# Batch 0 of a linear-attention and gated-FFN kernel worked in pairs of heads in place of halves, with a third of one weight loaded earlier

## The chip, the cores and the metric

The kernel runs on one core of a Trainium2 chip. The metric is the device time of one launch in microseconds (us), so lower is better. Five engines work side by side, each through its own list of instructions in a fixed order: TensorE (PE in the profile) multiplies matrices and transposes; VectorE (DVE) and ScalarE (ACT) work element by element; GpSimd (POOL) casts and issues the transfers of weights and of batches 1 to 7; SyncE (SP) issues the loads of batch 0 and the stores. Data moves between HBM and the on-chip SBUF by DMA; matmul results land in PSUM.

## The reference

Linear attention without softmax over 8 batches of 8 heads, 576 tokens and 64 channels, then a normalisation, then a gated feed-forward layer on the 4608 tokens of 512 channels. Inputs and output are 32-bit floats.

```python
# _attn_ref: q, k, v are (8, 8, 576, 64)
kv = np.einsum('bhsd,bhse->bhde', k, v)
out = np.einsum('bhsd,bhde->bhse', q, kv)
rms = np.sqrt(np.mean(out * out, axis=-1, keepdims=True) + 1e-06)
x = out / rms * g_norm                       # then heads side by side: (4608, 512)

# _moe_ref: w_gate, w_val (512, 1536); w_out (1536, 512); w_res (512, 512)
g = x @ w_gate
gelu = 0.5 * g * (1.0 + erf(g * inv_sqrt2))
val = x @ w_val
ffn_out = gelu * val @ w_out
res_gate = 1.0 / (1.0 + np.exp(-(x @ w_res)))
return x + res_gate * ffn_out
```

## The kernel before

Each batch gives a block of 512 tokens (4 tiles of 128, index j); its last 64 tokens ("rem", "last") are gathered, two batches to a tile, in a ninth block. A block's feed-forward part, which the slots below number, is twelve column blocks f of gate and value (`m_gval`), four residual tiles (`m_res`), and the product with w_out; in block 0 that product runs by twelve steps f over all four tiles (`out_by_f`). The attention of batch b + 1 is put amid the slots of block b. Batch 0 has nothing to hide behind: its q, k and v are loaded in two halves of four heads as 32-bit floats, cast on the engines, and worked through (k'v, q times it, norm, transposes) half after half, with the first two column blocks taken up as parts of x get ready (`first_gval`). Short matmuls on zeros (`keep_warm`) fill TensorE's waits. All other loads are cast in the transfer, issued by GpSimd in one row: weights of gate and value in four chunks of 256, 256, 512 and 512 columns, then w_res, batch 1, and w_out in thirds.

```python
    def load_batch(b):
        tiles_16(b)
        raw[b, "q"] = stage.tile([P, H, NJ * D], FP16, tag="qraw", name="qraw")
        raw[b, "k"] = stage.tile([P, H, NJ * D], FP16, tag="kraw", name="kraw")
        nc.gpsimd.dma_start(out=raw[b, "q"], in_=rows4(q, b, 0, H))
        nc.gpsimd.dma_start(out=raw[b, "k"], in_=rows4(k, b, 0, H))
        nc.gpsimd.dma_start(out=b16_t[b, "v"], in_=rows4(v, b, 0, H))
        load_last_kv(b)
        load_qr(b)
# ... (cut)
    def by_token(b, which):
        nc.vector.tensor_copy(
            out=b16_t[b, which].rearrange("p j h d -> p h j d"),
            in_=raw[b, which].rearrange("p h (j d) -> p h j d", j=NJ),
        )
# ... (cut)
    def load_wo(f0, f1):
        nc.gpsimd.dma_start(
            out=wo16[:, f0:f1, :], in_=moe_w_out[f0 * P : f1 * P, :].rearrange("(ff p) c -> p ff c", p=P)
        )
# ... (cut)
    def a_kv(b, lo, hi):
        if lo == 0:
            st[b]["kvp"] = pattn.tile([P, NP, P], FP32, tag="at", name="kvp")
        ps = st[b]["kvp"]
        for pr in range(lo, hi):
            kv_steps(b, ps[:, pr, :], pr)
        if hi == NP:
            nc.vector.tensor_tensor(
                out=st[b]["kv2"], in0=ps, in1=mask[:, None, :].to_broadcast([P, NP, P]), op=ALU.mult
            )

    def a_ss(b, j, ps):
        sq = attnp.tile([P, H, D], FP32, tag="sq", name="sq")
        nc.scalar.activation(out=sq, in_=ps, func=AF.Square)
        nc.vector.tensor_reduce(out=st[b]["ss"][:, j, :], in_=sq, op=ALU.add, axis=mybir.AxisListType.X)
# ... (cut)
    def a_o(b, j):
        s = st[b]
        ps = pattn.tile([P, C], FP32, tag="at", name="op")
        for pr in range(NP):
            nc.tensor.matmul(
                ps[:, pr * P : (pr + 1) * P], lhsT=s["qT"][:, j, pr, :], rhs=s["kv2"][:, pr, :], start=True, stop=True
            )
        a_ss(b, j, ps)
        s["o"][j] = ps
# ... (cut)
        nc.scalar.copy(out=qtr[0][:, :, 0:R], in_=ps[:, :, 0:R])
        nc.scalar.copy(out=qtr[1][:, :, R : 2 * R], in_=ps[:, :, R : 2 * R])

    def a_rem_o(b):
        # ... (cut: matmuls with both batches' kv2, copy, a_ss)
# ... (cut)
    def m_gval(blk, f):
        if f == 0:
            hids[blk] = hidp.tile([P, NF, NJ * P], FP16, tag="hid", name="hid")
        gps = pmoe.tile([P, NJ * P], FP32, tag="mm", name="gps")
        m_mm(gps, wg_c, f, blk, 0, NJ)
        vps = pmoe.tile([P, NJ * P], FP32, tag="mm", name="vps")
        m_mm(vps, wv_c, f, blk, 0, NJ)
        m_act(blk, f, gps, vps)
# ... (cut)
    def out_by_f(blk):

        ths, fpss, pfs = [], [], []
        slots = [lambda j=j: ths.append(m_res(blk, j)) for j in range(NJ)]

        def step(f):
            if f == 0:
                fpss.extend(pmoe.tile([P, C], FP32, tag="mm", name="fps") for _ in range(NJ))
            for j in range(NJ):
                m_ffn(blk, j, f, fpss[j])
            if f == NF - 1:
                pfs.extend(m_gate(ths[j], fpss[j]) for j in range(NJ))

        slots += [lambda f=f: step(f) for f in range(NF)]
        return slots, [lambda j=j: m_store(blk, j, pfs[j]) for j in range(NJ)]
# ... (cut)
    def load_first(which, t, half):
        hs = slice(half * HH, (half + 1) * HH)
        nc.sync.dma_start(out=raw[0, which][:, hs, :], in_=rows4(t, 0, hs.start, hs.stop))
# ... (cut)
    for half in range(2):
        load_first("q", q, half)
        load_first("k", k, half)
        load_first_last(0, half)
        load_first_last(1, half)
        load_first("v", v, half)
# ... (cut)
    def f_cast_last(half):
        hs = slice(half * HH, (half + 1) * HH)
        for i in range(2):
            nc.gpsimd.tensor_copy(out=last_kv[0][i][0:R, hs, :], in_=last_raw[i][:, hs, :])
# ... (cut)
    f_cast("q", 0, HH, nc.scalar.copy)
    f_qT(0)
    f_cast("k", 0, HH, nc.vector.tensor_copy)
    f_qT_out(0, nc.scalar.copy)
    f_qT_out(1, nc.scalar.copy)
    nc.vector.tensor_copy(out=g16, in_=gps)
    f_cast_last(0)
    f_cast("v", 0, HH, nc.vector.tensor_copy)
    keep_warm(7)
    f_kv(0)
    f_kv_out(0)
    f_cast("q", HH, H, nc.scalar.copy)
    keep_warm(2)
    f_o(0, 0, 2, pmoe, "mm")
    f_o(0, 2, 2, pmoe, "mm")

    hold = consts.tile([1, 1], FP16, name="hold")
    nc.gpsimd.tensor_copy(out=hold, in_=s0["kv2"][0:1, 0, 0:1])
    load_wg(0)
    load_wv(0)
    f_cast("k", HH, H, nc.gpsimd.tensor_copy)
    f_cast_last(1)
    for i in range(1, len(WCS)):
        load_wg(i)
        load_wv(i)
    f_sq(0, 0, 2)
    f_sq(0, 2, 2)
    f_red(0, 0, 2)
    # ... (cut: squares, sums, norm, transposes of the first half amid k'v of the second)
# ... (cut)

        hids[0] = hidp.tile([P, NF, NJ * P], FP16, tag="hid", name="hid")
        tiles = [pmoe.tile([P, NJ * P], FP32, tag="mm", name=n) for n in ("gps", "vps", "gps", "vps")]

        def part(j0, j1, c0, c1):
            for f in range(2):
                m_mm(tiles[2 * f], wg_c, f, 0, j0, j1, c0, c1)
                m_mm(tiles[2 * f + 1], wv_c, f, 0, j0, j1, c0, c1)

        part(0, 2, 0, 2)
        f_xT_pe(0, 2, 2)
        # ... (cut: the second half tile by tile, then the rest of the four products)
        for f in range(2):
            m_act(0, f, tiles[2 * f], tiles[2 * f + 1])
        load_qr(0)
# ... (cut)
        plan = {
            NF - 1: [lambda: by_token(b, "q")],
            NF: [lambda: by_token(b, "k")],
            NF + 3: [
                lambda: attn_begin(b),
                lambda: a_qT(b, 0),
                lambda: a_qT(b, 1),
                lambda: load_batch(b + 1),
                lambda: a_kv(b, 0, NP),
                lambda: a_rem_qT(b),
            ],
            NF + 4: [lambda: a_rem_o(b), o[0]],
            NF + 5: [o[1]],
            NF + 6: [o[2]],
            NF + 7: [o[3]],
            NF + 8: [lambda: a_norm(b), t[0], t[1], t[2], t[3], t[4]],
            2 * NF + 1: [x[0], x[1]],
            2 * NF + 2: [x[2], x[3]],
            2 * NF + 3: [x[4]],
        }
# ... (cut)
            if blk == 0 and s == 2:
                nc.gpsimd.dma_start(out=wr16, in_=moe_w_res.rearrange("(cc p) c -> p cc c", p=P))
                load_batch(1)
                for f in range(0, NF, 4):
                    load_wo(f, f + 4)
```

Of the kernel before, what the change touches and what calls it, by code (L numbers as in the profile page):

```python
# [18 lines left out]
def kernel(  # L19
# [15 lines left out]
    nc = tc.nc  # L35
# [391 lines left out]
    def load_first(which, t, half):  # L427
        hs = slice(half * HH, (half + 1) * HH)
        nc.sync.dma_start(out=raw[0, which][:, hs, :], in_=rows4(t, 0, hs.start, hs.stop))
# [11 lines left out]
    for half in range(2):  # L441
        load_first("q", q, half)
        load_first("k", k, half)
        load_first_last(0, half)
        load_first_last(1, half)
        load_first("v", v, half)
# [44 lines left out]
    def f_cast(which, lo, hi, copy):  # L491
        hs = slice(lo, hi)
# [9 lines left out]
    def f_cast_last(half):  # L502
        hs = slice(half * HH, (half + 1) * HH)
        for i in range(2):
            nc.gpsimd.tensor_copy(out=last_kv[0][i][0:R, hs, :], in_=last_raw[i][:, hs, :])

    def f_qT(half):
        q16 = b16_t[0, "q"].rearrange("p j h d -> p j (h d)")
        for e2 in range(2):
            pr = 2 * half + e2  # L510
            first["qT", pr] = ps = pattn.tile([P, NJ, P], FP16, tag="at", name="qtp")
            for j in range(NJ):
                nc.tensor.transpose(ps[:, j, :], q16[:, j, pr * P : (pr + 1) * P], ident)
# [4 lines left out]
    def f_kv(half):  # L518
        first["kv", half] = ps = pattn.tile([P, 2, P], FP32, tag="at", name="kvp")
        for e2 in range(2):  # L520
            kv_steps(0, ps[:, e2, :], 2 * half + e2)

    def f_kv_out(half):
        nc.vector.tensor_tensor(
            out=s0["kv2"][:, 2 * half : 2 * half + 2, :],
            in0=first["kv", half],
            in1=mask[:, None, :].to_broadcast([P, 2, P]),
# [3 lines left out]
    def f_o(half, j0, n, pool, tag):  # L531

        first["o", half, j0] = ps = pool.tile([P, n, HH * D], FP32, tag=tag, name="op")
        for j in range(n):
            for e2 in range(2):
                pr = 2 * half + e2
                nc.tensor.matmul(
                    ps[:, j, e2 * P : (e2 + 1) * P],
                    lhsT=s0["qT"][:, j0 + j, pr, :],
                    rhs=s0["kv2"][:, pr, :],  # L540
                    start=True,
                    stop=True,
                )

    def f_sq(half, j0, n):
# [295 lines left out]
```

## Time and profile before

The median of three runs is 356.24 us (356.02 to 356.77); the profiled execution spans 354.6 us.

| engine | busy us | share of the span | instructions |
|---|---|---|---|
| TensorE matmul | 343.0 | 97% | 1905 |
| TensorE weight load | 168.9 | 48% | 1905 |
| VectorE | 214.1 | 60% | 428 |
| ScalarE | 125.7 | 35% | 215 |
| GpSimd | 47.7 | 13% | 74 |

The page's lines name engine, source line and tiles as "out<-in". Busy time of TensorE's matmuls is modelled at its ends and overlaps from one to the next, so 97% is the share in which some matmul was under way, not a share of the peak. A table by stage gives for each stretch its length, then for PE, PE's weight loads, DVE, ACT and POOL the busy time and the instructions, then TensorE's granted clock (1.00 is full speed), the share of DMA engines busy (over 1 where two transfers overlap on an engine) and GB/s moved; bytes of a casting transfer are counted as written, at 16 bits. In the chain of waits each line has the start, the length and the instruction or transfer that held the end back.

### The profile page before, as it was taken

Reading aid. Unit: us, or ns where it says so; the run is one execution under the profiler, and the core shown is the slowest. Engines: PE = TensorE matmul, PEld = TensorE weight load, DVE = VectorE, ACT = ScalarE, POOL = GpSimd, SP = SyncE. Lnnn points to the kernel's source line nnn. Section 1 sums busy time; section 2 is a strip of 40 time slices with the busy share of each in tenths; the row PEclk is TensorE's granted clock in tenths of the full one; section 3 lists DMA queues with packets and bytes.
Section 4 is the critical chain, followed back from the end, with each engine's and each line's share of the span. In section 5 each row is a group of like instructions: output and inputs, shape, how many; then the busy total and the mean of one; then the engine's idle time right before and its main releaser. Section 6 shows DMA issues by size and latency. Waiting matters only on the chain.

```text
span 354.6 us, 5021 instructions
## 1 busy us (share of the span) xinstructions
PE 343.0 (97%) x1905; PEld 168.9 (48%) x1905; DVE 214.1 (60%) x428; ACT 125.7 (35%) x215; POOL 47.7 (13%) x74
## 2 busy tenths in 40 slices
PE   6879999999999999999999999999999999999995
PEld 2554465454454445544554445444544444444443
DVE  5655448868757774676569656865587543343433
ACT  3653474253146222531363125422542233223320
POOL 1853330050050005000130023000000000000000
PEclk9999999999999999999999999999999999999999
DMA  8999999489699058904594369327000500020013
GB/s 250 221 180 201 193 203 142 137 137 106 160 164 131 2 133 167 153 0 118 136 166 36 86 169 175 24 61 194 0 2 30 133 31 0 30 87 5 1 31 89
DMA packets 77707, 37.95 MB, mean 107 GB/s; under 512 B 42226, under 2 KB 73202, under 8 KB 77682
## 3 DMA queue, kind: packets, MB, share of 16 engines
q0 software_dynamic: 39792, 17.70, 39.7%
q1 hardware_dynamic: 37728, 19.80, 20.6%
q8 instruction: 15, 0.25, 0.3%
q10 hardware_dynamic: 162, 0.13, 0.1%
q14 instruction: 10, 0.08, 0.1%
HBM read 38.80 MB, written 9.44 MB: 136 GB/s over the span
## 4 chain that ended last, share of the span: by engine, by line
PE 84%; DMA 9%; POOL 2%; DVE 1%; SPq 1%; ACT 0%; issue 0%; DVEq 0%
PE fps L348 25%; PE gps L315 23%; PE vps L315 23%; PE rps L335 8%; DMA wv<-in_moe_w_val_dram 4%; DMA wo<-in_moe_w_out_dram 4%; PE op L194 2%; PE kvp L165 2%; DMA vf<-in_v_dram 1%; POOL wg L120 1%; PE fps L377 1%; POOL wv L120 1%; PE orp L212 1%; PE kvp L172 0%; SPq L435 0%; DVE hid L304 0%
## 5 line engine op out<-in xcount | busy, mean ns | idle before, releaser
L315 PE MATMUL gps<-xT,wg 128*128 128x512 f16 (+2 forms) x448 | 112.3, 371 | 2.3 <-ACT xT L597 1.2
L304 DVE TENSOR_TENSOR hid<-ge,vps 128x512 f16<-128x512 f16 x108 | 73.5, 685 | 65.8 <-PE vps L315 59.3
L315 PE MATMUL vps<-xT,wv 128*128 128x512 f16 (+2 forms) x448 | 112.3, 371 | 0.0
L303 ACT ACTIVATE ge<-gps 128x512 f16<-128x512 f32 x108 | 64.4, 598 | 114.3 <-PE gps L315 105.2
L348 PE MATMUL fps<-wo,hid 128*128 128x512 f16 x420 | 96.9, 379 | 0.6 <-DMA wo<-in_moe_w_out_dram 0.6
L315 PEld LDWEIGHTS <-wv 128*128 128x128 f16 x448 | 43.4, 98 | 50.4 <-DMA wv<-in_moe_w_val_dram 0.3
L348 PEld LDWEIGHTS <-hid 128*128 128x128 f16 x420 | 40.8, 98 | 48.7 <-DMA wo<-in_moe_w_out_dram 0.8
L315 PEld LDWEIGHTS <-wg 128*128 128x128 f16 x448 | 42.0, 98 | 44.0 <-issue 2.7
L354 DVE SCALAR_TENSOR_TENSOR pf<-th,fps 128x512 f32<-128x512 f32 x35 | 23.8, 686 | 47.6 <-PE fps L348 47.6
L344 ACT ACTIVATE th<-rps 128x512 f32<-128x512 f32 x36 | 21.5, 598 | 79.5 <-PE rps L335 79.5
L335 PE MATMUL rps<-wr,xT 128*128 128x512 f16 x144 | 36.5, 379 | 0.0
L188 DVE TENSOR_REDUCE ss<-sq 128x8 f32<-128x512 f32 x32 | 21.5, 683 | 7.3 <-ACT sq L187 5.5
L359 DVE SCALAR_TENSOR_TENSOR osb<-pf,t 128x512 f32<-128x512 f32 x35 | 24.2, 691 | 1.1
L335 PEld LDWEIGHTS <-xT 128*128 128x128 f16 x144 | 14.1, 98 | 17.0
L187 ACT ACTIVATE sq<-op 128x512 f32<-128x512 f32 x28 | 16.7, 598 | 9.9 <-PE op L194 9.2
L727 POOL COPY hold<-qT 1x1 f16<-1x1 f16 x5 | 0.9, 177 | 138.2 <-DMA qT<-q 138.2
L252 DVE TENSOR_TENSOR t<-op,ny 128x512 f16<-128x512 f32 x28 | 17.8, 680 | 0.1
L271 DVE TENSOR_TENSOR t<-t,g 128x512 f16<-128x512 f16 x36 | 13.3, 417 | 0.0
L165 PE MATMUL kvp<-v,k 128*128 128x128 f16 x128 | 10.6, 219 | 2.4 <-DVE v L495 2.2
L165 PEld LDWEIGHTS <-k 128*128 128x128 f16 x128 | 8.9, 98 | 6.3 <-DVE v L495 1.9
L194 PEld LDWEIGHTS <-qT 128*128 128x128 f16 x112 | 8.4, 98 | 5.7
L194 PE MATMUL op<-kv,qT 128*128 128x128 f16 x112 | 10.8, 219 | 0.0
(96 smaller groups left out, 168.0 us busy)
## 6 DMA issues: line engine op xcount, KB each, us to landing
out_dram<-osb SPq DMA_DIRECT2D x32, 256.0 KB, 2.4
qraw<-in_q_dram POOLq DMA_DIRECT2D x7, 512.0 KB, 6.1
kraw<-in_k_dram POOLq DMA_DIRECT2D x7, 512.0 KB, 8.3
v<-in_v_dram POOLq DMA_DIRECT2D x7, 512.0 KB, 10.1
wo<-in_moe_w_out_dram POOLq DMA_DIRECT2D x3, 512.0 KB, 14.0
qf<-in_q_dram SPq DMA_DIRECT2D x2, 512.0 KB, 4.7
kf<-in_k_dram SPq DMA_DIRECT2D x2, 512.0 KB, 5.8
vf<-in_v_dram SPq DMA_DIRECT2D x2, 512.0 KB, 6.0
```

Of the source, the lines that this page charges most:

```text
L165: nc.tensor.matmul(ps, lhsT=k16[:, j, cs], rhs=v16[:, 2 * pr : 2 * pr + 2, j * D : (j + 1) * D], start=(j == 0), stop=False,)
L188: nc.vector.tensor_reduce(out=st[b]["ss"][:, j, :], in_=sq, op=ALU.add, axis=mybir.AxisListType.X)
L194: nc.tensor.matmul(ps[:, pr * P : (pr + 1) * P], lhsT=s["qT"][:, j, pr, :], rhs=s["kv2"][:, pr, :], start=True, stop=True)
L252: nc.vector.tensor_tensor(out=t_t[blk][:, jj, :].rearrange("p (h d) -> p h d", h=H), in0=s["o"][j].rearrange("p (h d) -> p h d", h=H), in1 ...
L303: nc.scalar.activation(out=ge, in_=gps, func=AF.Gelu)
L304: nc.vector.tensor_tensor(out=hids[blk][:, f, :], in0=ge, in1=vps, op=ALU.mult)
L315: nc.tensor.matmul(ps[:, j0 * P : j1 * P], lhsT=w[:, cc, :], rhs=xT_t[blk][:, j0:j1, cc, :], start=(cc == 0 and j0 == 0), stop=(cc == NP - ...
L335: nc.tensor.matmul(rps, lhsT=xT_t[blk][:, j, cc, :], rhs=wr16[:, cc, :], start=(cc == 0), stop=(cc == NP - 1),)
L344: nc.scalar.activation(out=th, in_=rps, func=AF.Tanh, scale=0.5)
L348: nc.tensor.matmul(fps, lhsT=hids[blk][:, f, j * P : (j + 1) * P], rhs=wo16[:, f, :], start=(f == 0), stop=(f == NF - 1))
L354: nc.vector.scalar_tensor_tensor(out=pf, in0=th, scalar=1.0, in1=fps, op0=ALU.add, op1=ALU.mult)
L359: nc.vector.scalar_tensor_tensor(out=osb, in0=pf, scalar=0.5, in1=t_t[blk][:, j, :], op0=ALU.mult, op1=ALU.add)
```

## The change

Batch 0's q, k and v are loaded by pairs of heads (four pairs), and each step of its attention is done by pair, in an order written out as a row of words; a word names the step, the pair, for some the half of the token tiles (a or b), and the engine: qc, kc, vc and lc cast q, k, v and the last rows; qT and qo transpose q and copy it out; kv and kvo are k'v and its mask; o is q times it; sq, rd, rt, ri, t are square, sum, root, reciprocal and normalised x; xT and xo transpose x and copy it out; g and v are a pair's share of the first two gate and value column blocks; w issues a weight chunk, gelu loads ScalarE's table. So the norm of one pair runs beside the loads and casts of the next, and the first column blocks take up x pair by pair. The aim is that less work is left when the last of v has landed. GpSimd no longer waits for the first k'v before it issues weights, and casts parts of pair 2 itself. The first third of w_out is moved ahead of batch 1's loads, and the attention of batch 1 is put some slots later.

```diff
-    def load_first(which, t, half):
-        hs = slice(half * HH, (half + 1) * HH)
+    def load_first(which, t, pr):
+        hs = slice(2 * pr, 2 * pr + 2)
         nc.sync.dma_start(out=raw[0, which][:, hs, :], in_=rows4(t, 0, hs.start, hs.stop))
# ... (cut)
-    for half in range(2):
-        load_first("q", q, half)
-        load_first("k", k, half)
-        load_first_last(0, half)
-        load_first_last(1, half)
-        load_first("v", v, half)
+    for pr in range(NP):
+        load_first("q", q, pr)
+        load_first("k", k, pr)
+        if pr % 2 == 0:
+            load_first_last(0, pr // 2)
+            load_first_last(1, pr // 2)
+        load_first("v", v, pr)
# ... (cut)
+    tiles = {}
+    engines = {"A": nc.scalar.copy, "D": nc.vector.tensor_copy, "P": nc.gpsimd.tensor_copy}
+
+    def of_pair(pr):
+        return slice(2 * pr, 2 * pr + 2), slice(pr * P, (pr + 1) * P)
+
+    def f_cast(which, pr, copy):
# ... (cut)
+    def f_cast_last(half, copy):
         hs = slice(half * HH, (half + 1) * HH)
         for i in range(2):
-            nc.gpsimd.tensor_copy(out=last_kv[0][i][0:R, hs, :], in_=last_raw[i][:, hs, :])
-
-    def f_qT(half):
+            copy(out=last_kv[0][i][0:R, hs, :], in_=last_raw[i][:, hs, :])
# ... (cut)
+    def f_qT(pr):
         q16 = b16_t[0, "q"].rearrange("p j h d -> p j (h d)")
-        for e2 in range(2):
-            pr = 2 * half + e2
-            first["qT", pr] = ps = pattn.tile([P, NJ, P], FP16, tag="at", name="qtp")
-            for j in range(NJ):
-                nc.tensor.transpose(ps[:, j, :], q16[:, j, pr * P : (pr + 1) * P], ident)
+        first["qT", pr] = ps = pattn.tile([P, NJ, P], FP16, tag="at", name="qtp")
+        for j in range(NJ):
+            nc.tensor.transpose(ps[:, j, :], q16[:, j, of_pair(pr)[1]], ident)
# ... (cut)
+    def f_kv(pr):
+        first["kv", pr] = ps = pattn.tile([P, P], FP32, tag="at", name="kvp")
+        kv_steps(0, ps, pr)
+
+    def f_kv_out(pr):
+        nc.vector.tensor_tensor(out=s0["kv2"][:, pr, :], in0=first["kv", pr], in1=mask, op=ALU.mult)
# ... (cut)
+    def f_o(pr):
+        pool, tag = (pmoe, "mm") if pr < 2 else (pattn, "at")
+        first["o", pr] = ps = pool.tile([P, NJ, P], FP32, tag=tag, name="op")
+        for j in range(NJ):
+            nc.tensor.matmul(
+                ps[:, j, :], lhsT=s0["qT"][:, j, pr, :], rhs=s0["kv2"][:, pr, :], start=True, stop=True
+            )
+
+
+    def f_sq(pr, j0, j1):
+        first["sq", pr, j0] = sq = attnp.tile([P, j1 - j0, 2, D], FP32, tag=f"sq{j1 - j0}", name="sq")
+        ps = first["o", pr].rearrange("p j (h d) -> p j h d", h=2)
+        nc.scalar.activation(out=sq, in_=ps[:, j0:j1], func=AF.Square)
# ... (cut)
+    def f_mm(ws, i, pr, j0, j1):
+
+        for f in range(2):
+            if (f, i) not in tiles:
+                tiles[f, i] = [pmoe.tile([P, NJ * P], FP32, tag="mm", name="gv"[i] + "ps"), 0]
+            ps, done = tiles[f, i]
+            tiles[f, i][1] = done = done + j1 - j0
+            nc.tensor.matmul(
+                ps[:, j0 * P : j1 * P],
+                lhsT=w_of(ws, f)[:, pr, :],
+                rhs=xT0[:, j0:j1, pr, :],
+                start=(done == j1 - j0),
+                stop=(done == NP * NJ),
# ... (cut)
+    def f_piece(word):
+
+        name = word.rstrip("0123abADP")
+        rest = word[len(name) :]
+        # ... (cut: each word runs one step; "qc0A" casts q of pair 0 on ScalarE, D is VectorE, P is GpSimd)
# ... (cut)
+    opening = """
+    qc0A qT0 kc0D qo0A lc0P warm2 vc0D kv0 qc1A kvo0 kc1D o0 qT1 warm2 vc1D sq0 qc2P kv1 rd0 qo1A warm1 kvo1
+    kc2P rt0 qT2 o1 ri0 qo2D lc1P sq1 warm3 w0 t0 vc2A rd1 xT0 kv2 warm1 qc3A kvo2 qT3 rt1 o2 kc3D xo0A ri1 warm2
+    vc3D sq2 t1 w1 qo3A rd2 kv3 xT1 rt2 kvo3 o3 ri2 xo1A t2 sq3a sq3b g0 g1 rd3a rd3b
+    xT2 rt3 xo2D gelu v0 ri3 v1 g2 t3a xT3a t3b xT3b xo3aA xo3bD v2 g3a v3a g3b v3b
+    """
# ... (cut)
-    hold = consts.tile([1, 1], FP16, name="hold")
-    nc.gpsimd.tensor_copy(out=hold, in_=s0["kv2"][0:1, 0, 0:1])
-    load_wg(0)
-    load_wv(0)
-    f_cast("k", HH, H, nc.gpsimd.tensor_copy)
-    f_cast_last(1)
-    for i in range(1, len(WCS)):
-        load_wg(i)
-        load_wv(i)
# ... (cut)
+        for word in opening.split():
+            if word == "gelu":
                 nc.scalar.preload_act_table_set("gelu_and_others")
-            if j > 0:
-                part(j - 1, j, 2, NP)
-        part(NJ - 1, NJ, 2, NP)
+            else:
+                f_piece(word)
+        for i in range(2, len(WCS)):
+            load_wg(i)
+            load_wv(i)
         for f in range(2):
-            m_act(0, f, tiles[2 * f], tiles[2 * f + 1])
+            m_act(0, f, tiles[f, 0][0], tiles[f, 1][0])
# ... (cut)
-            NF - 1: [lambda: by_token(b, "q")],
-            NF: [lambda: by_token(b, "k")],
-            NF + 3: [
-                lambda: attn_begin(b),
-                lambda: a_qT(b, 0),
-                lambda: a_qT(b, 1),
-                lambda: load_batch(b + 1),
-                lambda: a_kv(b, 0, NP),
-                lambda: a_rem_qT(b),
-            ],
-            NF + 4: [lambda: a_rem_o(b), o[0]],
-            NF + 5: [o[1]],
-            NF + 6: [o[2]],
-            NF + 7: [o[3]],
-            NF + 8: [lambda: a_norm(b), t[0], t[1], t[2], t[3], t[4]],
+            NF + 3: [lambda: attn_begin(b), lambda: by_token(b, "q")],
+            NF + 4: [lambda: by_token(b, "k")],
+            NF + 5: [lambda: a_qT(b, 0), lambda: a_qT(b, 1), lambda: load_batch(b + 1)],
+            NF + 7: [lambda: a_kv(b, 0, NP), lambda: a_rem_qT(b), lambda: a_rem_o(b), o[0], o[1], o[2]],
+            NF + 8: [o[3]],
+            NF + 9: [lambda: a_norm(b), t[0], t[1], t[2], t[3], t[4]],
# ... (cut)
+                load_wo(0, 4)
                 load_batch(1)
-                for f in range(0, NF, 4):
+                for f in range(4, NF, 4):
```

## The prediction

> **What bounds the kernel now.** I read the page first: its rows of slices show where TensorE is not full, and DMA beside it.
>
> ```profile
> PE   6879999999999999999999999999999999999995
> ...
> DMA  8999999489699058904594369327000500020013
> ```
>
> One slice is 8.9 us. TensorE is short of full only in the first three slices and the last; transfers are dense through the first six. So the second view is a table by stage, cut where TensorE's steady matmuls begin (23.35 us) and where block 1 begins (60.21 us).
>
> ```profile
> 0.00:23.35 23.35, 16.76 (x146) 10.36 (x146) 13.32 (x41) 12.79 (x22) 13.13 (x24) 1.00 1.04 218
> 23.35:60.21 36.86, 36.21 (x228) 18.86 (x228) 20.70 (x43) 17.07 (x30) 9.84 (x13) 1.00 1.40 195
> 60.21:350.00 289.79, 289.65 (x1531) 139.56 (x1530) 179.18 (x343) 95.87 (x165) 24.73 (x37) 1.00 0.48 87
> ```
>
> After 60.21 us TensorE (first number after the length) lacks 0.14 us of 290. From there the kernel is a solid block of matmuls, and the change touches none of it. What the change is worth is therefore how much earlier **block 1 starts**; 60.21 us is the number to move. The third view is the chain of waits up to there.
>
> ```profile
> 3.25 5.09 DMA vf<-in_v_dram
> ...
> 18.01 14.18 DMA wv<-in_moe_w_val_dram
> ...
> 33.14 13.88 DMA wo<-in_moe_w_out_dram
> 47.07 1.04 PE fps L348 x4
> ...
> 58.90 1.27 ACT xT L265 x2
> 60.21 1.02 PE gps L315 x4
> ```
>
> It runs through transfers: v of batch 0, the last weight chunk, then w_out. Asked one issue at a time, the DMA view gives the landings: last half of v 6.51+6.9 = 13.4 us; wv chunk 1 at 15.09+5.8 = 20.9; wg chunk 2 at 15.82+8.8 = 24.6; wv chunk 2 at 16.55+10.6 = 27.15; wv chunk 3 at 32.2; batch 1's q 37.9, k 40.5, v 43.2, its last v rows 44.2; first third of w_out 33.14+13.9 = 47.0. These follow at some 2.55 us per 512 KB: one saturated stream. TensorE asked for wv chunk 2 at 27.66, half a microsecond after it landed, and waited 0.60 us for w_out at 47.07. **A faster opening alone therefore runs into the weights.** The fourth view is that stream around the weights.
>
> ```profile
> 14.00:15.50 1.50, 1.26 (x15) 0.99 (x15) 1.40 (x6) 0.00 (x1) 1.50 (x3) 1.00 1.25 164
> 15.50:17.00 1.50, 1.36 (x14) 0.93 (x14) 1.11 (x4) 1.50 (x3) 1.50 (x3) 1.00 0.92 94
> 17.00:19.00 2.00, 1.22 (x15) 1.01 (x13) 1.90 (x6) 1.32 (x4) 2.00 (x4) 1.00 1.39 182
> 19.00:20.50 1.50, 1.05 (x16) 0.89 (x14) 1.08 (x4) 0.47 (x1) 1.50 (x3) 1.00 0.91 104
> 20.50:22.00 1.50, 1.50 (x28) 1.37 (x26) 0.35 (x1) 1.07 (x2) 1.42 (x2) 1.00 1.19 184
> ```
>
> The last number is GB/s. Two holes: 94 and 104 against about 175. They cost 1.5 x (1 - 94/173) + 1.5 x (1 - 104/183) = 0.7 + 0.65 = 1.35 us of transfer time. GpSimd issued chunk 0 at 10.49 and 11.38 us, then cast k and the last rows (12.13 to 14.40), and only then issued chunk 1: the holes follow that break.
>
> **What the Trainium skill says.** "DMA: Bandwidth & Descriptors", section "SWDGE vs HWDGE vs iDMA": a DMA issued from GpSimd has its descriptors computed by GpSimd itself before an engine moves bytes. The trace agrees with the consequence, since GpSimd's busy break is followed by a hole; that descriptors are its cause isn't shown. The same page, "Rules for kernel authors": queues of different issuers run on the same 16 DMA engines and interleave. The trace agrees: the last v half took 6.9 us with weights beside it, the first 5.1. "TensorE: Matmul & The Clock Gate", "Architectural detail: the array is 16× 32×32, not 1× 128×128": VectorE and ScalarE are strictly first in, first out, so the position of a step in the new order is a wait. "ScalarE: Activation LUTs", "What ACT_TABLE_LOAD costs", gives 1283 ns for the load; the trace has 1.28 us, and the change puts it in the middle of the last pair's chain.
>
> **The change, part by part.**
>
> *Loads by pairs.* Ten issues on SyncE become sixteen, at some 0.5 us for q, k, v and 0.7 for the last rows (0.46 to 0.81 now): about 9 us of issuing, and the bytes are the same. The stream was full at some 300 GB/s, so the last v lands as before, 13.2 us (weights start a little later, which helps; the extra issues take a little). What gains is the earlier data: pairs 0 to 2 are through most of their norm by 13 us.
>
> *The chain after the last v.* Durations are from the groups by form, smaller tiles scaled from them (a quarter of the heads: cast of 128x512 from 0.69 for 1024, about 0.36; 128x256 forms as measured). Cast to 13.6. VectorE's order then has t of pair 1 (0.68) and the sum of pair 2 (0.68) ahead of the mask of pair 3: 14.95, mask 0.27, o3 0.3: 15.55. ScalarE still has the 0.69 copy of pair 1 to do, then two squares of 0.42: 16.8. Sum of the second half 0.36: 17.2. Sqrt 0.30, reciprocal 0.19: 17.8. t in two halves of 0.42: 18.65. The table load starts after the sqrt at 17.55 and holds ScalarE to 18.85, so its copy of x' (0.47) ends 19.3. Four to eight short matmuls: 20.0. Gelu of the first tile 0.60, which frees the PSUM buffer: f = 2 starts at **20.65 us against 23.35**. From the last v that is 7.4 us in place of 9.9.
>
> *Weights.* The last rows of k and v of heads 4 to 7 now stand after three pairs of q and k and two of v, 0.5 MB earlier: about 10.3 us. GpSimd casts them (0.4 each) and starts chunk 0 at about 11.2, 0.7 later than now, but then issues all eight back to back: chunk 2 at about 14.4 against 15.8. If only the two holes close, wv chunk 2 lands at 27.15 - 1.35 = 25.8; if the rest of the ramp (184 against 201 GB/s later) improves as well, at 24.4. I take 25.1. TensorE wants it at 20.65 + 3 x 1.728 - 0.86 = 24.97 (a column block of g and v is eight matmuls, 1.728 us, from 24.21 to 25.94 and on). It waits 0.15 us. Block 0's residual matmuls end at 25.1 + 0.86 + 7 x 1.728 + 3.46 = 41.5 us; call this T. Now T is 44.07, and 0.6 of waiting comes on top.
>
> *w_out's first third ahead of batch 1.* It lands at about 35.2 + 2.55 - 2 = 36, so step 0 at T no longer waits. Batch 1 is pushed back by 2.55 and pulled forward by the shift of 1.5 to 2: its last rows land at about 45.0. That is why batch 1's attention is put later.
>
> *The later attention.* Two steps, the q transposes, two steps, then k'v: 4 x 0.864 + 0.89 = 4.35 us after T, so 45.85 us instead of 44.91. From there the order is dense: k'v ends 1.3 us on, mask and copies of the remainder's q 0.8, then o of the remainder and three more at once. TensorE idles about 0.9 us there, which it did not. Five sums of 0.67 on VectorE end 7.15 us after k'v began (8.5 now, where the o are spread over steps). Norm and four t then take 5.12 us (53.39 to 58.51 now): 12.3. Last transposes, step 11 and the fifth transposes: **block 1 starts 13.6 us after k'v begins, against 15.3**. TensorE waits some 1.9 us for t ahead of step 10, since all twelve steps no longer stand between.
>
> *Sum.* 45.85 + 13.6 = 59.45 against 60.21: 0.75 us earlier. Of the 2.7 us won in front, 2.0 is given back as TensorE's idle time in batch 1's attention. 356.24 - 0.75 = **355.5 us**.
>
> **The rivals.** *All of the front shows*: 2.7 us, 353.5. For it: TensorE does the same work, and 60.21 on is solid. Against: VectorE's chain of sums, norm and t (9.4 us from first sum to last t now) hangs on k'v, and k'v moves later, not earlier. *The weights don't move*: wv chunk 2 at 27.15 makes T 43.5, k'v 47.9 and block 1 61.5, so 357.5. For it: the bytes are the same and chunk 0 is issued later. Against: the two holes. *Batch 1 is the limit*: with no shift its last rows land at 44.2 + 2.55 = 46.75, block 1 at 60.35: 356.4. For it: transfers are dense to 58 us. Against: the same holes. *VectorE or ScalarE becomes the bound of the opening*: VectorE is busy 13.3 of 23.35 us and the pairs add fixed costs; a step out of place by 1 us moves T by 1 us, unless the weights hide it.
>
> **Range and chances.** The three terms with play are the weights (1 us either way), the opening's order (0.7) and the dense attention (0.7). They add to the same T and k'v, and partly hide one another: 354.0 to 356.9 us. A change of 2% is 7 us; the whole opening before steady matmuls is 23 us, of which 13.4 is loading, so either side has about one chance in a hundred.
>
> **What would show it.** In the changed profile: last v cast near 13.2 us; first 128x512 matmuls of f = 2 near 20.7; weight issues back to back and no hole between 15 and 20 us; a small wait at wv chunk 2; no wait for w_out; k'v of batch 1 near 45.9; new idle time of TensorE of about 1 us ahead of the remainder's o and 2 us ahead of the transposes of batch 1's x; block 1 at 59.4. I am wrong if f = 2 starts after 22 us, if wv chunk 2 lands after 26 us, or if TensorE doesn't stop for t.

## The result, and the profile after

The changed kernel takes 360.11 us (median of 4 runs, 358.99 to 361.30) against 356.37 us for the kernel before: a ratio of 1.0105, 95% interval 1.0059 to 1.0150. The change costs about 3.7 us, where a gain of 0.75 was forecast.

The page's rows of slices (8.9 us each) show TensorE full from the fourth slice on, but for the seventh. The first three look better than before.

```profile
PE   8899997999999999999999999999999999999995
...
DMA  7999999279479047903593279417000500020013
```

TensorE is busier in front; the dent in the seventh slice (53.6 to 62.5 us) is new. The table by stage, cut where steady matmuls begin and where block 1 begins, has the columns of the table before: length, busy time of PE, its weight loads, DVE, ACT and POOL, the clock, the DMA share, GB/s.

```profile
0.00:22.33 22.33, 19.25 (x111) 9.86 (x111) 14.19 (x45) 12.29 (x23) 12.08 (x24) 1.00 0.98 213
22.33:62.73 40.40, 36.96 (x229) 18.71 (x228) 20.80 (x43) 17.30 (x30) 10.42 (x14) 1.00 1.34 187
62.73:352.50 289.77, 289.63 (x1530) 139.50 (x1530) 179.21 (x343) 95.95 (x165) 24.75 (x37) 1.00 0.48 87
```

Steady matmuls begin 1.02 us sooner (22.33 for 23.35), but block 1 begins 2.52 us later (62.73 for 60.21). The span of this run is 357.2 against 354.6 us, so this shift is the whole loss of this run, and from there on the block is as solid as before. TensorE stands idle for 3.44 of the 40.40 us of the middle stage, against 0.65 of 36.86 before. The chain of waits says where.

```profile
5.92 5.76 DMA kf<-in_k_dram
11.68 0.05 issue
11.73 0.62 POOL k L504
12.35 0.34 POOL kl L512
12.69 0.34 POOL vl L512
13.03 0.84 POOL wg L120
...
16.79 10.64 DMA wv<-in_moe_w_val_dram
27.43 0.05 issue
27.48 1.04 PE vps L315 x4
...
62.73 1.02 PE gps L315 x4
```

The chain no longer starts at v. It runs through k of pair 2, three casts of GpSimd in a row behind it, the weights that GpSimd issues only after those casts, and weight chunk 2, which lands at 27.43. (In the part left out it runs on through matmuls, then k'v, the sums and the norm of batch 1.) TensorE's timeline shows the stops; the bracket is the idle time ahead and what ended it.

```profile
27.48 1.04 PE L315 MATMUL vps<-xT,wv 128*128 128x512 f16 x4 [0.67 <-DMA wv<-in_moe_w_val_dram]
...
43.89 2.09 PE L348 MATMUL fps<-wo,hid 128*128 128x512 f16 x8
...
48.43 0.39 PE L165 MATMUL kvp<-v,k 128*128 128x128 f16 x4
...
50.40 0.84 PE L212 MATMUL orp<-kv,qtr 128*128 128x128 f16 x8 [0.47 <-ACT qtr L205]
...
59.30 0.40 PE L264 MATMUL xtp<-ident,t 128*128 128x128 f16 x4 [1.98 <-DVE t L252]
```

There is a wait for weight chunk 2, a short one for the remainder's q, and nearly 2 us for t of batch 1. The same points in the kernel before:

```profile
44.07 1.06 PE L155 MATMUL qtp<-ident,q 128*128 128x128 f16 x16
...
44.96 0.39 PE L165 MATMUL kvp<-v,k 128*128 128x128 f16 x4
```

From before to after the shift adds up as follows. The residual matmuls end (T in the prediction) and the first step of w_out comes at 43.89 us; it waits for nothing (w_out landed at 38.08). Before, T was 44.07, followed by a 0.6 us wait for w_out after k'v. k'v of batch 1 starts 4.54 us after T, at 48.43 (before: 0.89 after it, at 44.96), and block 1 starts 14.30 us after k'v (before 15.25). So -0.18 + 3.65 - 0.95 = 2.52 us.

The four runs lie on two levels: 358.99 and 359.04 us at a mean TensorE clock of 0.997, 361.17 and 361.30 at 0.993 and 0.990. The profiled run is one of the lower pair, so its 2.6 us explains that level only. The remaining 2.2 us of the upper level are taken up below.

### The profile page after: what moved, and what is told of

Same layout as the page of the kernel before. It is cut to its first block, busy times and chain, and to the rows that moved or that the text cites. A ratio compares the mean times of both kernels' runs of the same rounds, so it can differ in the third digit from the quotient of the medians.

```text
span 357.2 us, 4957 instructions
## 1 busy us (share of the span) xinstructions
PE 346.2 (97%) x1870; PEld 168.2 (47%) x1870; DVE 215.1 (60%) x432; ACT 125.5 (35%) x216; POOL 47.3 (13%) x74
## 4 chain that ended last, share of the span: by engine, by line
PE 87%; DMA 5%; DVE 3%; POOL 1%; SPq 1%; ACT 1%; issue 0%; DVEq 0%; ACTq 0%
PE vps L315 25%; PE gps L315 24%; PE fps L348 24%; PE rps L335 9%; DMA wv<-in_moe_w_val_dram 3%; PE kvp L165 2%; DMA kf<-in_k_dram 2%; PE op L194 2%; SPq L429 1%; PE fps L377 1%; POOL wg L120 1%; PE orp L212 1%; DVE ss L188 1%; ACT sq L187 0%; PE kvp L172 0%
## 5 line engine op out<-in xcount | busy, mean ns | idle before, releaser
L315 PE MATMUL vps<-xT,wv 128*128 128x512 f16 x424 | 108.8, 379 | 0.7 <-DMA wv<-in_moe_w_val_dram 0.7
L315 PE MATMUL gps<-xT,wg 128*128 128x512 f16 x424 | 108.8, 379 | 0.4 <-ACT ge L303 0.4
L315 PEld LDWEIGHTS <-wv 128*128 128x128 f16 x424 | 41.4, 98 | 51.0 <-DMA wv<-in_moe_w_val_dram 1.2
L315 PEld LDWEIGHTS <-wg 128*128 128x128 f16 x424 | 39.9, 98 | 41.8 <-issue 0.5
L165 PE MATMUL kvp<-v,k 128*128 128x128 f16 x128 | 11.2, 224 | 0.7 <-DVE v L502 0.5
```

The lines of the kernel that those rows point to most:

```text
L165: nc.tensor.matmul(ps, lhsT=k16[:, j, cs], rhs=v16[:, 2 * pr : 2 * pr + 2, j * D : (j + 1) * D], start=(j == 0), stop=False,)
L315: nc.tensor.matmul(ps[:, j0 * P : j1 * P], lhsT=w[:, cc, :], rhs=xT_t[blk][:, j0:j1, cc, :], start=(cc == 0 and j0 == 0), stop=(cc == NP - ...
```

## The experiments

My first theory was this: GpSimd's casts of pair 2 hold the weights, which eats the gain in front, and the later attention of batch 1 then costs its full price. The rivals were that loads of 256 KB are slower and make everything late, that the cold clock in the opening is at fault (the trace lists the granted clock in records of one value each; the first record of full clock begins at 13.68 us, before at 3.97), and that w_out ahead of batch 1 is at fault.

### One part put back or taken alone: e1 to e4

**e1, loads by halves.** Batch 0 is loaded in 512 KB pieces again; the work stays by pairs.

```diff
-        hs = slice(2 * pr, 2 * pr + 2)
+        hs = slice(pr * HH, (pr + 1) * HH)
# ... (cut: the loop runs over two halves, as in the kernel before)
```

> The changed kernel with batch 0 loaded by halves as before (ten loads, not sixteen); all steps still by pair. Theory 'small loads' (loads by pair move slower, so the last v and with it GpSimd's weight issues come late): last v cast near 13.5 us instead of 15.2, first weight issue near 11.7 instead of 13.0, wv chunk 2 landing near 26 instead of 27.4, step 0 of w_out (T) near 42.4 instead of 43.9, block 1 near 61.2, time about 1.5 us under the changed kernel. Rival 'cold clock' (TensorE runs its first 13.7 us at half speed, with fewer warming matmuls): T stays at 43.9 and the time within 0.4 us.

Measured: 360.58 us, ratio 1.0114 (1.0090 to 1.0139). The last v does land sooner, at 13.65 against 15.16 us: for the same bytes, sixteen loads took 1.5 us longer than ten. All of it is lost in the first half of the bytes: up to the v of pair 1, or of the first half, they had landed at 9.93 us in sixteen loads and at 8.45 in ten, and the second half took 5.2 us in both. But k of the second half lands at 11.42, so GpSimd still issues its first weight only at 12.79 (12.97 in the changed kernel); chunk 2 lands at 27.96, and block 1 starts at 63.26. Nothing is won. Slower small loads are real, but here they are not what holds the weights. What faster loads would be worth to work done by pair, this run doesn't show: with data in halves the last cast of v starts only at 16.29 and f = 2 at 23.63.

**e2, a warm TensorE.** More matmuls on zeros in the opening, nothing else.

```diff
-    keep_warm(5)
+    keep_warm(7)
# ... (cut: likewise 3 to 6, and the "warm" words about doubled)
```

> The changed kernel with more warming matmuls (7 for 5 at the start, 6 for 3, and about twice as many between the first pairs); nothing else. 'Cold clock': zero matmuls at about 0.22 us apart from 4 us on, f = 2 begins before 21.5 us instead of 22.3, and the times of single runs, 359.0 and 361.2 for the changed kernel, fall together near 358.5 or under. 'Small loads': last v cast stays at 15.2 us and wv chunk 2 at 27.4, so T stays at 43.9 and the fast runs at 359.

Measured: 360.24 us, 1.0114 (1.0087 to 1.0140). The first record of full clock now begins at 9.11 us, and the time does not fall. But f = 2 begins at 23.94, later than without the added matmuls (22.33), so this run alone doesn't settle it. The run e8 below does: its opening is the changed kernel's, word for word; its first record of full clock begins at 9.00 us for 13.68, and f = 2 at 22.41, T at 43.70. The cold opening is not the cause. The trace of e2 also holds a stretch at half clock from 60.31 to 63.73 us, right behind a stop of TensorE from 58.19 to 60.17: the first sign of the upper level.

**e3, the late attention alone.** The kernel before, with only the order of w_out and the place of batch 1's attention taken from the changed kernel.

```diff
+            NF + 3: [lambda: attn_begin(b), lambda: by_token(b, "q")],
+            NF + 4: [lambda: by_token(b, "k")],
+            NF + 5: [lambda: a_qT(b, 0), lambda: a_qT(b, 1), lambda: load_batch(b + 1)],
+            NF + 7: [lambda: a_kv(b, 0, NP), lambda: a_rem_qT(b), lambda: a_rem_o(b), o[0], o[1], o[2]],
+            NF + 8: [o[3]],
+            NF + 9: [lambda: a_norm(b), t[0], t[1], t[2], t[3], t[4]],
# ... (cut)
+                load_wo(0, 4)
                 load_batch(1)
```

> The kernel before with only the first third of w_out moved ahead of batch 1 and batch 1's attention put later. Theory 'late attention' (the later order costs by itself what the profile shows after T): T at 44.1 without a wait, k'v at 48.5, TensorE idle about 1 us ahead of the remainder's o and 2 us ahead of the transposes, block 1 at 62.6, time 2.3 us over the kernel before. Rival (the loss comes from the opening): within 0.5 us of the kernel before.

Measured: 360.10 us, 1.0107 (1.0080 to 1.0133). Without a single pair in it, this kernel loses as much as the change, and more than the 2.3 us expected. Its timeline has the same two stops:

```profile
50.86 0.84 PE L212 MATMUL orp<-kv,qtr 128*128 128x128 f16 x8 [0.46 <-ACT qtr L205]
...
59.75 0.40 PE L264 MATMUL xtp<-ident,t 128*128 128x128 f16 x4 [1.98 <-DVE t L252]
```

w_out's first step starts at 44.35 without a wait, k'v at 48.89, 4.54 us later as in the changed kernel. Its runs lie on the same two levels, 359.27 and 359.62 us at a clock of 0.998, 360.58 and 360.83 at 0.993. The profiled run is one of the upper pair, and here the table of windows, cut at the bounds of the clock's records, shows the price (the second number is TensorE's busy time, the third from the end its clock):

```profile
57.32:60.74 3.42, 1.24 (x12) 0.56 (x10) 3.11 (x10) 0.55 (x1) 0.00 (x0) 1.00 1.54 147
60.74:64.15 3.41, 3.41 (x16) 1.74 (x14) 1.84 (x4) 2.00 (x4) 0.00 (x0) 0.50 0.06 4
```

The stop falls wholly into one record, and the next 3.41 us run at half clock. From the first transposes behind the stop to block 1 takes 4.90 us here (59.75 to 64.65) and 3.43 in the changed kernel's profiled run (59.30 to 62.73), so the half clock cost 1.47 us.

**e4, the pairs alone.** The changed opening, with the old order of w_out and the old place of the attention (the reverse of the diff of e3, in the changed kernel).

> The changed kernel with w_out and batch 1's attention in the old order; only the opening by pairs is left. 'Late attention': TensorE waits for w_out at about 47 us as before, block 1 near 60.3, time within 0.6 us of the kernel before. Rival (the loss comes from the opening): 2 us or more over the kernel before.

Measured: 357.73 us (12 runs), 1.0044 (1.0028 to 1.0061): 1.50 us over the kernel before, between what the theory and the rival had said. The first weight is issued at 13.13, chunk 2 lands at 27.77, w_out at 48.23 (before 47.02); k'v is as before (45.12), but then TensorE waits 1.66 us for w_out, and block 1 starts at 61.43. Block 1 is 1.2 us late, as late as w_out. e3 and e4 do not add up (3.87 + 1.50 us against 3.74 for both): e3's order removes the wait on w_out in which e4's delay shows.

### The stream of weights: e5 and e6

**e5, the kernel before, without the break in GpSimd's issues.** The second half's cast of k moves to VectorE.

```diff
-    f_cast("k", HH, H, nc.gpsimd.tensor_copy)
# ... (cut)
+    f_cast("k", HH, H, nc.vector.tensor_copy)
```

> The kernel before with one cast moved: k of heads 4 to 7 is cast on VectorE ahead of the v cast, not on GpSimd between weight chunks 0 and 1; GpSimd then issues chunk 1 at about 13.0 us instead of 14.4. Theory 'issue break' (the holes at 15.5 and 19 us come from GpSimd's break): the first hole closes, wv chunk 2 lands near 26.1 instead of 27.1 and the first third of w_out near 46.0, TensorE no longer waits for it, block 1 near 59.7, time 0.5 us under the kernel before. Rival (the stream is full and the holes come from the transfers themselves): w_out at 47.0, time within 0.15 us.

Measured: 356.20 us (21 runs), 0.9994 (0.9987 to 1.0000). That is 0.27 us under the kernel before, at the edge of the noise, where I had expected 0.5. The hole at 15.5 us closes (193 GB/s for 94), and another opens ahead of it (112 GB/s at 13 to 14 us). Chunk 2 lands at 26.62 and w_out at 46.50, half a microsecond sooner, and the wait for w_out is gone; but v is cast later and block 1 starts at 60.34. What the hole was worth is not settled: runs with the old opening unchanged have chunk 2 land at 26.37 (e7), 26.91 (e12), 27.14 (before) and 27.31 us (e3). The 1.35 us or more that I had read off it did not come.

**e6, the pairs with the weights first.** e4, with chunk 0 issued before GpSimd's cast of k of pair 2.

```diff
-... vc1D sq0 qc2P kv1 rd0 ... sq1 warm3 w0 t0 ...
+... vc1D sq0 qc2P w0 kv1 rd0 ... sq1 warm3 t0 ...
```

> The opening by pairs with w_out and batch 1's attention in the old order, as in the run with the opening alone, and chunk 0 of the weights issued right after GpSimd's cast of q of pair 2, ahead of its casts of k of pair 2 and the last rows. Theory 'late weights' (the opening by pairs loses because GpSimd's casts hold the weights back): first weight issue near 11.4 us instead of 13.1, wv chunk 2 near 26.4 instead of 27.8, w_out near 46.9 instead of 48.2, block 1 near 60.2, time 1.2 us under the run with the opening alone, so level with the kernel before. Rival (the loads by pair make the stream itself longer): w_out stays near 48, time stays at 1.5 us over the kernel before.

Measured: 356.61 us (20 runs, 355.03 to 357.26), 0.9994 (0.9983 to 1.0004). GpSimd's timeline of this run:

```profile
10.85 0.90 POOL L120 DMA_DIRECT2D wg<-in_moe_w_gate_dram  x1
11.74 0.77 POOL L120 DMA_DIRECT2D wv<-in_moe_w_val_dram  x1
12.48 0.64 POOL L504 CAST k<-kf 128x512 f16<-128x512 f32 x1
```

One word moved brings the first weight from 13.13 to 10.85 us, chunk 2 from 27.77 to 25.74, w_out from 48.23 to 45.61, and the median from 1.50 to 0.14 us over the kernel before. This shows that late weights were a fault of the opening. It doesn't make the opening a gain: the median is level with the kernel before. In the profiled run (355.08 us) block 1 starts at 58.81, 1.4 us before the old start; but that run is one of the three fastest of twenty, and only it has a trace. In it no weight chunk holds TensorE behind f = 2, which begins at 22.18, and T is 42.90:

```profile
42.90 1.06 PE L155 MATMUL qtp<-ident,q 128*128 128x128 f16 x16
```

No run joins these early weights with the late attention. From the changed kernel's distances block 1 would start at about 42.90 + 4.54 + 14.30 = 61.74 us (an estimate), still later than before.

### What the late attention costs: e7, e8, e10

**e7, w_out ahead, nothing else.** The kernel before with only the one line `load_wo(0, 4)` ahead of `load_batch(1)`.

> The kernel before with only the first third of w_out ahead of batch 1; batch 1's attention stays where it was. If the order of the transfers is what costs (batch 1 lands 2.5 us later and its chain ends last): TensorE stops 2 us at k'v, which begins near 46.9 (last rows of v) to 47.4, block 1 near 62, time 1.8 to 2.5 us over the kernel before. If only the later place of the attention costs: k'v near 45, within 0.5 us of the kernel before.

Measured: 356.82 us (12 runs), 1.0014 (1.0004 to 1.0025). I had expected a stop of 2 us at k'v; TensorE waited 0.20 us for the last rows of v, and block 1 started at 60.08. In that run the weights happened to land early (chunk 2 at 26.37), and it is the lowest of the twelve; but the median too is only 0.35 us over before. e3 differs from this kernel in nothing but the later place of the attention, so with the old opening it is that place that costs.

**e8, the stop filled.** The changed kernel, with eight matmuls on zeros added into an accumulator ahead of the transposes of batch 1's x. They add nothing to the sum and leave nothing out.

```diff
+    def fill():
+        for _ in range(8):
+            nc.tensor.matmul(fill_into[0], lhsT=zeros[:, 0:P], rhs=zeros, start=False, stop=False)
# ... (cut)
-            2 * NF + 1: [x[0], x[1]],
+            2 * NF + 1: [fill, x[0], x[1]],
```

> The changed kernel with eight matmuls of zeros added into the w_out sum ahead of batch 1's transposes, where TensorE stood idle for 2.0 us; nothing else, and the sum is unchanged. Theory 'idle halves the clock' (the 2 us of idle time, when they fall into one stretch of 3.4 us, halve TensorE's clock for the next 3.4 us, which parts the single runs into 359 and 361): no half-clock stretch near 60 us in the records, and all runs within 0.6 us of 359.0. Rival (the two levels have another cause): runs at 361 stay.

Measured: 359.58 us (6 runs, 358.80 to 360.19; clocks 0.997 to 1.0), 1.0081 (1.0068 to 1.0093). The upper level is gone: no run is above 360.2, no mean clock below 0.997, and the profiled run has no half-clock record there. Three of the six lie more than 0.6 us above 359.0, so the runs do not fall together as closely as I had expected. First the windows of the changed kernel, cut at the bounds of its records:

```profile
54.64:58.05 3.41, 2.67 (x13) 1.00 (x11) 2.97 (x13) 0.54 (x1) 0.00 (x0) 1.00 1.46 198
58.05:61.46 3.41, 1.97 (x21) 1.33 (x22) 3.27 (x7) 1.33 (x3) 0.00 (x0) 1.00 1.39 124
```

And those of this kernel, the second starting just behind the stop that is now filled:

```profile
56.78:60.20 3.42, 2.97 (x20) 1.36 (x19) 3.11 (x11) 0.66 (x2) 0.00 (x0) 1.00 1.67 187
60.20:63.61 3.41, 3.37 (x25) 1.88 (x24) 3.19 (x7) 2.58 (x6) 0.00 (x0) 1.00 0.36 27
```

The eight matmuls on zeros are 1.89 of the 2.97 us in the first of these. Without them that record would hold about 1.1 us of work (an estimate), less than the one in e3.

In the profiled run of the changed kernel the same 2 us stop happened to fall across a bound, leaving 2.67 and 1.97 us busy, and the clock stayed full. In e3, it fell into one record (1.24 us busy) and the clock was halved; in e2, likewise (1.43). The lower level remains in e8, with block 1 at 62.54: the waiting itself, which filling can't shorten.

**e10, the changed kernel with the attention back at its old place.** Pairs and w_out ahead stay.

```diff
-            NF + 7: [lambda: a_kv(b, 0, NP), lambda: a_rem_qT(b), lambda: a_rem_o(b), o[0], o[1], o[2]],
+            NF + 3: [ ... lambda: a_kv(b, 0, NP), lambda: a_rem_qT(b)],
# ... (cut: the rest of the old plan)
```

> The changed kernel with only batch 1's attention put back where it was; loads and steps by pair and w_out ahead stay. Theory 'late attention': k'v begins at about 45.3 to 47 us (batch 1's last rows) instead of 48.4, no idle 2 us ahead of the transposes, block 1 near 60.7, no run at half clock near 60 us, time 2 to 2.8 us under the changed kernel. Rival (the transfers' order costs it): k'v waits past 47 us and block 1 stays above 62.

Measured: 358.88 us (4 runs), 1.0074 (1.0055 to 1.0092), 2.74 us over the kernel before, where the changed kernel is 3.74 over: a gain of 1.0, less than I had expected. k'v now waits 1.22 us for v of batch 1 and 0.40 us for its last rows, and starts at 46.64; block 1 starts at 61.84. With w_out ahead and the weights late, batch 1 lands late (v at 46.60), so the old place isn't free either: e4, with w_out in its old order too, is only 1.50 over. With the pairs, the late place and the order of w_out both seem to cost, but the intervals of the three ratios overlap, so the sizes are rough. One half-clock record, from 12.30 to 15.72 us, lies in this run's opening; its share isn't separated, but the run is the fastest of the four.

### A version that gains: e9, e11, e12

**e9.** e6, with the last rows of k and v loaded from ScalarE's queue at the start, so that GpSimd casts them early and SyncE has twelve loads.

```diff
-        nc.sync.dma_start(
+        nc.scalar.dma_start(
             out=last_raw[i][:, hs, :], ...
# ... (cut)
-... sq0 qc2P w0 kv1 ... kc2P rt0 qT2 o1 ri0 qo2D lc1P sq1 ... t1 w1 qo3A ...
+... sq0 lc1P qc2P w0 kv1 ... kc2P w1 rt0 qT2 o1 ri0 qo2D sq1 ... t1 qo3A ...
```

> The opening by pairs with the old order of w_out and attention and early weights, and besides: the four loads of the last rows of k and v are issued by ScalarE at the start, so SyncE issues twelve loads and no others; GpSimd casts the last rows early and issues chunk 1 right after its cast of k of pair 2. Theory 'thin stream at the start' (SyncE's sixteen issues leave the transfers short at 4 to 6 us, and the last rows hold GpSimd up): last v lands near 14.0 us instead of 14.8, first weight issue near 10.2 instead of 10.85, f = 2 near 21.3 instead of 22.2, block 1 near 58.0, time 0.8 us under the run with chunk 0 first, 1.0 us or more under the kernel before. Rival (256 KB transfers are slower each, whoever issues them): last v at 14.8 or later, time as the run with chunk 0 first.

Measured: 356.16 us (13 runs), 0.9998 (0.9990 to 1.0007), level with the kernel before, where I had expected 1.0 us under it. The last v lands at 14.37, f = 2 starts at 21.83, k'v at 43.56, all a little sooner than in e6; but w_out lands at 46.79 and TensorE waits 1.78 us for it, so block 1 starts at 59.99. Its first weight is issued at 11.15, where I had hoped for 10.2. k'v is 1.4 us ahead of the old kernel's, and TensorE waits it away.

**e11.** That wait is filled with work that was due anyway: o of the remainder and of three pairs moves ahead of w_out's first step, and the norm three slots sooner.

```diff
+                lambda: a_rem_o(b),
+                *o[0:3],
             ],
-            NF + 4: [lambda: a_rem_o(b), o[0]],
-            NF + 5: [o[1]],
-            NF + 6: [o[2]],
-            NF + 7: [o[3]],
-            NF + 8: [lambda: a_norm(b), t[0], t[1], t[2], t[3], t[4]],
+            NF + 4: [o[3]],
+            NF + 5: [lambda: a_norm(b), t[0], t[1], t[2], t[3], t[4]],
```

> The run with the last rows on ScalarE's queue, and batch 1's remainder and first three o put ahead of step 0 of w_out, where TensorE waited 1.8 us for it; norm two slots earlier. Theory 'the wait can be filled' (w_out's landing bounds the front, and the norm of batch 1 hangs on the o): k'v still at 43.6, step 0 at 46.9 with little wait, last sum near 50.7, no wait for t, block 1 near 58.6 instead of 60.0, time 1.3 us under the kernel before. Rival (VectorE's chain or the transfers set block 1 whatever the order): within 0.3 us of the kernel before.

Measured: 355.51 us (19 runs) against 356.36, ratio 0.9978 (0.9971 to 0.9986). A gain of 0.2%, small but clear of the noise. Its chain of waits:

```profile
46.84 0.67 PE op L194 x12
47.51 0.86 PE fps L348 x4
48.38 0.22 PE op L194 x4
48.60 7.77 PE fps L348 x36
...
59.26 1.02 PE gps L315 x4
```

w_out has left the chain: it landed at 46.40 while TensorE did the o, and its steps run without a stop from 47.35. Block 1 starts at 59.26, 0.95 us before the old start, and 0.85 us is what the median gains. I had expected 58.6; but apart from 0.55 us ahead of the remainder's o TensorE no longer waits here, so its own work bounds the steps, and k'v of batch 1 came no sooner than 43.95.

**e12.** The same order of the attention in the kernel before.

> The kernel before with the same denser attention of batch 1 and nothing else. If the gain of the run beside it needs the earlier opening: TensorE reaches step 0 at about 48.3 instead of 47.1 and finishes block 0 no earlier, block 1 near 60.0, time within 0.4 us of the kernel before. If the order alone gives it: 1 us or more under the kernel before.

Measured: 356.74 us (22 runs), 1.0009 (1.0000 to 1.0018). There k'v starts only at 45.66, and w_out's first step, behind the o, only at 49.07, where w_out had been ready at 47.02; block 1 starts at 60.98. Some 0.7 us of that is a late opening in this one run (the same opening had k'v at 44.96 in the kernel before), but the median of 22 runs says the same: the order alone gains nothing. It takes the earlier opening to make it fit.

## Why the prediction was wrong, step by step

*What bounds the kernel*: right. Block 1's start is the number to move, and in the changed kernel's profiled run its shift (2.52 us) is the loss (2.6 us).

*"The last v lands as before, 13.2 us"*: wrong by 2 us. It lands at 15.16 and its cast starts at 15.18. Bytes and stream rate were the argument, and the number of issues was taken as nearly free; by e1, the cut into sixteen loads accounts for 1.5 us of it. The prediction also took the 6.9 us of the last half of v, against 5.1 for the first, as a sign that weights beside it slow a load. But e1, whose first weight is issued only at 12.79, less than a microsecond before v lands, has 7.1 and 5.2 us: that difference is there almost without weights.

*"From the last v that is 7.4 us"*: right. From the start of the last v cast to f = 2 is 7.15 us. The chain's length was read well; f = 2 came at 22.33 rather than 20.65 because the chain began late.

*"Starts chunk 0 at about 11.2"*: **the step on which the front failed.** It was 12.97. I put the last rows at 10.3 us; they landed at 12.17 and 12.53, late with the whole stream of batch 0. And I left out that the same GpSimd must first cast k of pair 2, which landed at 11.68 and kept it until 12.3. In its order it could issue nothing before these casts; the last rows alone would have held it to about 12.9 us (12.53 and a cast of 0.34, an estimate), so the cast of k adds next to nothing here. The holes did close as predicted, with all eight issues in a row from 12.97 to 19.0 (174 and 176 GB/s from 15 to 20.5 us), though one of 95 GB/s opened at 14 to 15 us, and after issue the time to landing was as before (10.64 against 10.6 us for chunk 2). But closing them brought at most a fraction of the 1.35 us counted (e5), and the late start cost more. Chunk 2 landed at 27.43, not 25.1; the predicted wait of 0.15 us became 0.67; T, the start of w_out's first step, was 43.89 in place of 41.5. So the front gained 0.18 us in place of 2.6. e6 changes only when chunk 0 is issued, and the loss falls from e4's 1.50 us to 0.14: this cause is shown.

Early weights alone would not have brought T to 41.5, because the late v stands behind them as a second limit. From f = 2 TensorE needs ten column blocks and the residual matmuls, 10 x 1.728 + 3.46 = 20.74 us. With f = 2 at 22.33, T can't come before 43.07; e6, with no weight in the way, has f = 2 at 22.18 and T at 42.90. Of the 2.4 us by which T missed, the weights hold about 0.8 and the late v about 1.6.

*w_out's first third*: right that step 0 no longer waits. It landed at 38.08 us, 2 us later than predicted, as the weights ahead of it did.

*The later attention*: right in kind, a little short in size. k'v came 4.54 us after T (4.35 predicted); the stops were 0.47 and 1.98 us (0.9 and 1.9 predicted). Block 1 came 14.30 us after k'v, for 13.6: the sums end 7.48 us after k'v, for 7.15, and the end of four t to block 1 takes 1.70 us, for 1.33. The second figure could have been read from before, where it is 60.21 - 58.51 = 1.70 us.

*The sum*: "of the 2.7 us won in front, 2.0 is given back". The giving back came to 2.70 us (3.65 - 0.95) and the winning did not come: -0.18 + 2.70 = 2.52. e3 shows that the giving back happens without any change in front. Against the forecast for block 1 (59.45) the miss is 3.28 us: 2.39 from T, 0.19 from T to k'v and 0.70 from k'v to block 1. A cost that comes without the gain had been joined to a gain that rested on an assumed stream.

*Not foreseen at all*: the clock. The predicted stop of about 2 us was counted at its length, when in part of the runs it also halves the clock behind it (e2, e3 in the records; e8 by removal) and costs 1.3 (e2) to 1.5 us (e3) more. The Trainium skill, "TensorE: Matmul & The Clock Gate", "What's actually happening", describes a window of 3413 ns that runs freely and isn't set by the kernel's start. The traces agree: the half-clock records are 3.41 us long, and whether one follows the stop differs from run to run. The same page, "HAM oscillation — how this bites in real kernels", gives as a rule that gaps above about 3.4 us are to be avoided. Here 1.98 us was enough where it fell into one record, so the measurement decides.

*The rivals*: "the weights don't move" was nearest, with k'v at 47.9 and block 1 at 61.5 (measured 48.43 and 62.73). I set it aside because of the two holes. Its mark, "wv chunk 2 lands after 26 us", was among those I named as showing me wrong, and so was "f = 2 starts after 22 us".

*What stays open.* Why 256 KB pieces take longer is not shown: a cost per transfer is the plain reading of sixteen against ten, but nothing here isolates it. In e9, with four of the sixteen issued by ScalarE, the last v landed at 14.37 us. The upper level of the changed kernel's own runs has no trace; its halved clock is concluded from their mean clocks and from e2, e3 and e8. Nor does one half record explain all of it: the levels lie 2.2 us apart, and such a record cost 1.3 to 1.5. A low mean clock can also come from the opening, as in e10. T itself varies between runs with the same opening, from 44.07 to 44.77 us with the old one (before, e3, e7, e12) and from 43.70 to 44.37 with the changed one (e8, the changed kernel, e4, e10), so the 0.18 us says only that the front gained little. The landing of the weights varies by about a microsecond between kernels with the same issues, and probably makes the spread of e6, which is only argued.

## What to carry to other kernels

When work is cut finer so that it starts sooner, follow each engine that also issues transfers: a cast given to it waits for its own data, and everything it was to issue waits behind (here the first weight, to 13.13 us in e4 for 10.85 in e6). A step that gives time back on purpose must be priced by itself, as e3 was, because it costs its full price when the gain it counts on fails. And a stop of TensorE like the one of 1.98 us here is to be priced with the half clock that may follow it (1.3 to 1.5 us), or the order chosen so that due work fills it, as in e11.

## What the runs showed of the hardware

- One record of half clock, 3.41 us, followed where TensorE was busy for 1.24 us (e3), 1.43 us (e2) or 1.65 us (e10, in the opening) of the record before it; with 1.79 us (e1), 1.97 us (changed kernel) or 2.97 us (e8) busy it did not. Busy time alone doesn't draw the line: near the end of e6 a record with 1.45 us busy (347.53 to 350.94) is followed by one of full clock.
- The same bytes of batch 0 had landed after 13.65 us in ten loads (e1) and after 15.16 us in sixteen (changed kernel).
- With one and the same opening, full clock was reached at 13.68 us (changed kernel) or at 9.00 (e8), and f = 2 began at 22.33 and 22.41: TensorE's clock isn't what the opening waits for. With the old opening it was reached at 3.97 (before) or 9.54 (e3), and f = 2 began at 23.35 and 23.63.
